# Attention and GEGLU in one kernel: padding fills and normalisation tails moved to GpSimd, three reorderings in the first block, and another form of the closing test

## The chip, the cores and the metric

The kernel runs on one core of a Trainium2 chip. The metric is the device time of one execution in microseconds (us). The engines are called as the profile has them: PE is TensorE, DVE VectorE, ACT ScalarE, POOL GpSimd, SP SyncE, whose queue issues nearly all DMAs.

## The reference

The input x has 2048 rows of 448, all in bf16. It is normalised row by row and goes through two branches whose results are added to it.

```python
xn = layernorm(x)
# A: 16 heads of 28, causal sliding window of 256 keys
q, k, v = split(xn @ wqkv)
p = softmax(where(0 <= i - j < 256, q @ k.T * 28 ** -0.5, -1e9))
# B: F = 1792
h = gelu(xn @ w_gate) * (xn @ w_up)
return x + (p @ v) @ wo + h @ w_down
```

## The kernel before

The rows are worked on in four query blocks (qb 0 to 3) of 512 rows, that is four tiles of 128 rows each. A block goes through attention, then through the gate and up projections (`gated`), and its down projections, to which the attention's output projection is added in the same PSUM tile, run inside the next block's attention. The order of all instructions is written out by hand: the program emits them one after another, and each engine takes its own in that order. While PE works on a block's attention, generators (`Feed`, `share`) put the projections of the next block and other matmuls in between, by a cost in ns that each yields.

Block 0 is special, since nothing is there yet when it begins. Its attention has twelve steps, three for each of the four head groups g. A step computes scores on PE, takes their Exp on ACT (`p_sb`), and zeroes the parts outside the window with selects on POOL (`masked`). A group's PV product (`pv(g)`) comes ahead of the scores of steps 4, 7 and 10, and after the last step for the fourth group; it needs the masked `p_sb` of that group's three steps. The score tile is single-buffered here (`score_pool(1)`), so a step's scores wait until the Exp before them has read it.

Between block 0's steps stand the q and k projections of groups 1 to 3 (`gen_qk`), the last two v tiles of the block, early up projections, and block 1's projections. A list `aux` has one entry for each step: normalisation of tiles 4 to 7 and their DMA transposes (`ahead`, `ahead2`, `ahead3`), then `fill_pads`, then statistics of tiles 8 to 11. `stat` computes mean and variance on DVE, `rstd` the reciprocal root on ACT as Exp(-0.5 Ln), `norm` scales a tile in two pieces, 448 columns and a copy of the last 64 (the tail).

The contraction of 448 is three chunks of 128 and a half chunk of 64. The half chunks of two products use both halves of PE's rows and run side by side: q with k (`qk_halves`, weights `w3p`), and v of two tiles (`v_half`).

Heads have 28 columns in places of 32. In the free four columns of the padded weights `wqp`, `wkp` and `w3p` the later blocks compute the keys of head group 3; `fill_pads` writes the weights for that, by twelve copies of 16 or 48 elements a partition and a memset.

The PV product also gives the row sums of the softmax. `sums` transposes them into rows, copies them into `l_all` and takes their reciprocal; `inverse` transposes that back, and `scale_o` multiplies on POOL. At the end the program tests that all sums lay within 1e-18 and 1e18, adds the 128 partitions' answers up in a matmul (`nok`), and reads the count as a register of every engine; a second, general path would run if it were not 128. That matmul, the copy of its result and the register load stand among the last block's down projections.

Of the kernel before, what the change touches and what calls it, by code (L numbers as in the profile page):

```python
# [9 lines left out]
ALU = mybir.AluOpType  # L10
AX = mybir.AxisListType
bf16 = mybir.dt.bfloat16
f32 = mybir.dt.float32
i32 = mybir.dt.int32

S, D, H, Dh, F = 2048, 448, 16, 28, 1792
P = 128
NT = S // P
NF = F // P
QB, NB = 512, 4  # L20
SCALE = float(Dh) ** -0.5
L_LO, L_HI = 1e-18, 1e18


HOLD = True
# [29 lines left out]
def share(feeds, first, second):  # L55

    want = [first, second]
    while True:
        can = [i for i, f in enumerate(feeds) if f.gens and want[i] > 190 and not f.held]
        if not can:  # L60
            return
        i = max(can, key=lambda i: (not feeds[i].closed, want[i]))
        for f in feeds:
            if f is not feeds[i]:
                f.closed = False
        want[i] -= feeds[i].run()


def drain(feeds):

    while any(f.gens for f in feeds):
        min((f for f in feeds if f.gens), key=lambda f: (f.held, f.closed)).run()
# [3 lines left out]
def kernel(  # L76
# [11 lines left out]
    nc = tc.nc  # L88
    const = ctx.enter_context(tc.tile_pool(name="const", bufs=1))
# [3 lines left out]
    work = fast.enter_context(tc.tile_pool(name="work", bufs=3))  # L93
# [3 lines left out]
    phase = [None]  # L97
# [84 lines left out]
    kT = const.tile([P, 4, S], bf16, name="kT")  # L182
    mv_all = const.tile([P, NT, 2], f32, name="mv_all")
    rstd_all = const.tile([P, NT], f32, name="rstd_all")
    l_all = const.tile([P, NB * 4, 16], f32, name="l_all")

    def warmup(n):
        wps = phase[0].pool.tile([P, 2, QB], f32, name="wps", tag="s")
# [9 lines left out]
    def rstd(t, n):  # L198
        lnv = work.tile([P, 4], f32, name="lnv")
        nc.scalar.activation(out=lnv[:, 0:n], in_=mv_all[:, t:t + n, 1], func=ACT.Ln, bias=eps_t[:, 0:1], scale=1.0)  # L200
        nc.scalar.activation(out=rstd_all[:, t:t + n], in_=lnv[:, 0:n], func=ACT.Exp, scale=-0.5)
# [3 lines left out]
    def norm(t):  # L205
        xn = work.tile([P, 4, P], bf16, name="xn", bufs=4)
        xf = xn[:, :, :].rearrange("p a b -> p (a b)")
        for eng, lo, n, src in ((nc.vector, 0, D, 0), (nc.gpsimd if t in (1, 2) else nc.vector, D, 64, 384)):
            eng.tensor_scalar(out=xf[:, lo:lo + n], in0=x_sb[:, t, src:src + n], scalar1=mv_all[:, t, 0:1],
                              scalar2=rstd_all[:, t:t + 1], op0=ALU.subtract, op1=ALU.mult)  # L210
        xns[t] = xn
# [38 lines left out]
    def v_half(t, pv):  # L250
        mm_half(pv, xnT[:, 3, t * P:(t + 1) * P], wv[:, 3, :], t % 2, False, True)
# [22 lines left out]
    def qk_halves(qb, g, pq, pk):  # L274
        w3 = w3p[:, 4 * g:4 * g + 4, :].rearrange("p h d -> p (h d)")
        for hi, ps in enumerate((pq, pk)):
            mm_half(ps, w3, xnT[:, 3, qb * QB:(qb + 1) * QB], hi, False, True)
# [7 lines left out]
    def gen_qk(qb, gs, others=()):  # L285

        for g in gs:
            pq = bank("pq")[:, :]
            proj(pq, wqp, qb, g)
            if qb and g == 3:  # L290
                yield 650
                ts = slice(qb * QB, (qb + 1) * QB)
                nc.tensor.matmul(pq, lhsT=w3p[:, 12:16, :].rearrange("p h d -> p (h d)"), rhs=xnT[:, 3, ts], start=False, stop=True,
                                 skip_group_check=True)
                nc.scalar.copy(out=qT[:, 3, ts], in_=pq)
                done.add((qb, 3))
                yield -220
                return
            yield 650
            pk = bank("pk")[:, :]  # L300
            proj(pk, wkp, qb, g)
            yield 650, HOLD
            qk_halves(qb, g, pq, pk)
            for t, pv in others:
                v_half(t, pv)
            if others:
                v_copy(*others[1], nc.vector.tensor_copy)
            qk_copies(qb, g, pq, pk)
            others = ()
            yield -360  # L310

    def fill_pads(last):


        def put(dst, src, n, lo):

            src = src.rearrange("p (j d) -> p j d", d=Dh)[:, :, lo:]
            if n == 4:
                nc.vector.tensor_copy(out=dst[:, 12:16, Dh:32], in_=src[:, :, 24:28])
            src = src[:, :, 0:24].rearrange("p j (g i) -> p g j i", i=8)[:, :, :, 0:4]  # L320
            nc.vector.tensor_copy(out=dst[:, 0:12, Dh:32].rearrange("p (g j) i -> p g j i", j=4), in_=src)

        if not last:
            for c in range(3):
                k = wraw[:, c, D + 12 * Dh:2 * D]
                put(wqp[:, c, :, :], k, 4, 0)
                put(wkp[:, c, :, :], k, 3, 4)
            return
        put(w3p[0:64, :, :], w3k[0:64, :], 4, 0)
        put(w3p[64:128, :, :], w3k[64:128, :], 3, 4)  # L330
        nc.vector.memset(w3p[64:128, 12:16, :], 0.0)

    k3 = dram.tile([4, 7, 4, QB], bf16, name="k3")

# [17 lines left out]
    DOWN = 4 * 3400  # L352
# [178 lines left out]
    def attention(qb, feeds, aux, plan):  # L531
# [7 lines left out]
        def sums():  # L539

            g, oc = copied.pop(0)
            l1 = work.tile([P, 16, 32], f32, name="l1", tag="wc", bufs=1)
            ls = l_all[:, 4 * qb + g, :]
            nc.vector.transpose(out=l1[:, :, :].rearrange("p a b -> p (a b)"), in_=oc[:, :])  # L544
            nc.vector.tensor_copy(out=ls, in_=l1[:, :, Dh])
            ri = work.tile([P, 16], f32, name="ri")
            nc.vector.reciprocal(out=ri[:, :], in_=ls)
            inverses.append((g, oc, ri, l1))

        def inverse():  # L550

            g, oc, ri, l1 = inverses.pop(0)
            rb = l1 if qb else work.tile([P, 16, 32], f32, name="rb", tag="wb", bufs=1)
            nc.vector.transpose(out=rb[:, :, :], in_=ri[:, :].unsqueeze(2).to_broadcast([P, 16, 32]))  # L554
            later.append((g, oc, rb[:, :, :].rearrange("p a b -> p (a b)")))

        def add_halves(oc, ov):
# [33 lines left out]
        for i, (scores, ncol, edges) in enumerate(steps):  # L591
# [18 lines left out]
            for g, half, kt, q0, nq, col in scores:  # L610
                k0, nk = (64 * half, 64) if half is not None else (0, P)
                for j in range(4):
                    r = slice(32 * j, 32 * j + Dh)
                    nc.tensor.matmul(ss[k0:k0 + nk, j, col:col + nq], lhsT=kT[r, g, kt * P + k0:kt * P + k0 + nk],  # L614
                                     rhs=qT[r, g, qb * QB + q0:qb * QB + q0 + nq], start=True, stop=True,
                                     tile_position=(32 * j, k0), skip_group_check=True)
                parts.setdefault(g, []).append((half, kt, q0, nq, col, p_sb))
            nc.scalar.activation(out=p_sb[:, :, 0:ncol], in_=ss[:, :, 0:ncol], func=ACT.Exp, scale=SCALE)  # L618
            flush()
            if qb:  # L620
# [106 lines left out]
    def ahead2():  # L727
        stat(6)
        stat(7)
        rstd(6, 2)  # L730
        norm(5)
        dma_transp(5)

# [74 lines left out]

    g1 = work.tile([P, 512], f32, name="g1", tag="wc", bufs=1)
    g2 = work.tile([P, 512], f32, name="g2", tag="wb", bufs=1)  # L810
    okc = const.tile([P, 1], f32, name="okc")
    okb = const.tile([P, 1], bf16, name="okb")
    one = const.tile([P, 1], bf16, name="one")
    lf = l_all[:, :, :].rearrange("p a b -> p (a b)")
    nc.vector.memset(one[:, :], 1.0)
    nc.vector.tensor_scalar(out=g1[:, 0:256], in0=lf, scalar1=L_LO, scalar2=None, op0=ALU.is_ge)
    nc.vector.scalar_tensor_tensor(out=g2[:, 0:256], in0=lf, scalar=L_HI, in1=g1[:, 0:256], op0=ALU.is_le, op1=ALU.mult)
    nc.vector.tensor_reduce(out=okc[:, :], in_=g2[:, 0:256], axis=AX.X, op=ALU.min)
    nc.vector.tensor_copy(out=okb[:, :], in_=okc[:, :])
    feed = Feed((gen_down(NB - 1, "dmomd" if last_tag[0] == "o" else "omdmo"), DOWN))  # L820
    share([feed], DOWN / 3, 0)
    nok = phase[0].pool.tile([P, 2 * QB], f32, name="nok", tag="s")
    nc.tensor.matmul(nok[0:1, 0:1], lhsT=okb[:, :], rhs=one[:, :], start=True, stop=True)
    flag = const.tile([1, 1], i32, name="flag")
    nc.vector.tensor_copy(out=flag[:, :], in_=nok[0:1, 0:1])
    share([feed], DOWN / 3, 0)
    n_ok = nc.values_load(flag[0:1, 0:1], min_val=0, max_val=P)
    drain([feed])
    phase[0].close()
    fast.close()  # L830


    with tc.If(n_ok < P, preferred_fallthrough_block=True, label="general"):
        general_path(tc, locals_=dict(x_sb=x_sb, xnT=xnT, qT=qT, kT=kT, v_sb=v_sb, wg=wg, wu=wu, wgu3=wgu3, wd=wd, wo=wo,
                                      ident=ident, outv=outv))

# [108 lines left out]
```

## Time and profile before

| | us |
|---|---|
| median of 3 runs | 222.42 |
| lowest and highest | 222.25, 222.54 |
| the profiled execution | 222.38 |
| its span | 220.7 |
| PE busy | 210.7 (95%) |
| DVE busy | 156.2 (71%) |
| ACT busy | 133.3 (60%) |
| POOL busy | 44.7 (20%) |

The span goes from the first instruction to the last; what lies around it belongs to the time. Busy shares are means over the span. The program is one long pipeline with a start of some 12 us, in which the first tiles come in and are normalised.

### The profile page before, as it was taken

The numbers are of one execution on the slowest core, as the hardware profiler recorded it, in microseconds if no ns is written. First come the engines' busy times: TensorE is split into PE (matmuls) and PEld (weight loads), VectorE is DVE, ScalarE is ACT, GpSimd is POOL, SyncE is SP. The second block draws the span as 40 slices with busy tenths as digits, with TensorE's granted clock in tenths as the row PEclk, the third lists the DMA queues.
The fourth block names the chain that finished last, engine by engine and source line by source line (L and its number), as shares of the span: only waits on it lengthen the run. The fifth ranks groups of instructions, "written<-read, shape, count | busy, mean of one in ns | idle before, by whom it ended". The sixth has DMA issues, their size and how long they took to land.

```text
span 220.7 us, 5415 instructions
## 1 busy us (share of the span) xinstructions
PE 210.7 (95%) x2257; PEld 95.2 (43%) x2282; DVE 156.2 (71%) x370; ACT 133.3 (60%) x131; POOL 44.7 (20%) x65
## 2 busy tenths in 40 slices
PE   6899999999999999999999999999999999999992
PEld 1333333443444454434444445443344445444472
DVE  5989996799666993679565796396345899579320
ACT  3587788662878875432878887233576777564000
POOL 5763687320000120022000022022000022022000
PEclk9999999999999999999999999999999999999999
DMA  6999799203200001102300000200000000000010
GB/s 190 283 296 98 142 344 301 66 1 73 46 0 24 24 24 27 20 0 47 72 1 24 23 0 24 50 16 0 0 4 21 24 3 24 24 1 0 22 46 25
DMA packets 18045, 13.30 MB, mean 60 GB/s; under 512 B 8704, under 2 KB 16992, under 8 KB 18016
## 3 DMA queue, kind: packets, MB, share of 16 engines
q1 hardware_dynamic: 17072, 12.62, 22.7%
q8 instruction: 19, 0.31, 0.6%
q10 hardware_dynamic: 944, 0.29, 0.5%
q14 instruction: 10, 0.08, 0.2%
HBM read 9.15 MB, written 2.18 MB: 51 GB/s over the span
## 4 chain that ended last, share of the span: by engine, by line
PE 91%; DVE 4%; DMA 1%; issue 1%; ACT 0%
PE po L376 20%; PE gt L228 15%; PE u L228 12%; PE sc L614 6%; PE po L371 6%; PE gt L234 5%; PE ue L228 5%; PE ov L574 5%; PE pq L228 4%; PE pv L228 4%; PE pk L228 3%; PE pq L234 2%; DVE st L195 2%; PE g L228 1%; DMA x_sb<-in_A_x_dram 1%
## 5 line engine op out<-in xcount | busy, mean ns | idle before, releaser
L618 ACT ACTIVATE p_sb<-sc 128x2048 bf16<-128x2048 f32 (+2 forms) x42 | 73.8, 1758 | 12.6 <-PE sc L614 7.2
L376 PE MATMUL po<-wd,hT 128*128 128x448 bf16 (+1 forms) x238 | 50.0, 342 | 0.0
L459 ACT ACTIVATE ge<-gt 128x1024 bf16<-128x1024 f32 x26 | 26.6, 1024 | 34.9 <-PE u L234 20.1
L537 POOL TENSOR_TENSOR oN<-oc,l 128x512 bf16<-128x512 f32 x12 | 16.0, 1332 | 137.5 <-DVE l L554 87.2
L228 PE MATMUL gt<-xnT,wg 128*128 128x512 bf16 x149 | 36.1, 379 | 1.0 <-issue 1.0
L466 DVE TENSOR_TENSOR hT<-ge,u 128x512 bf16<-128x512 bf16 x40 | 25.7, 682 | 11.9 <-ACT ge L459 11.8
L376 PEld LDWEIGHTS <-hT 128*128 128x128 bf16 x238 | 21.4, 98 | 18.6 <-issue 2.6
L228 PE MATMUL u<-xnT,wu 128*128 128x512 bf16 x116 | 29.0, 379 | 0.2
L518 DVE TENSOR_TENSOR p_sb<-p_sb,masks 128x256 bf16<-128x256 bf16 (+1 forms) x90 | 27.3, 357 | 0.4 <-ACT p_sb L618 0.4
L228 PEld LDWEIGHTS <-wg 128*128 128x128 bf16 x168 | 15.3, 98 | 21.3 <-issue 4.5
L228 PEld LDWEIGHTS <-wu 128*128 128x128 bf16 x168 | 16.0, 98 | 19.2 <-issue 1.0
L559 DVE TENSOR_TENSOR oc<-oc,ov 128x512 f32<-128x512 f32 x12 | 8.2, 687 | 15.2 <-ACT oc L558 15.2
L614 PE MATMUL sc<-qT,kT 28*64 28x320 bf16 (+7 forms) x640 | 16.9, 263 | 0.1
L381 DVE TENSOR_TENSOR res<-po,x_sb 128x448 bf16<-128x448 f32 (+1 forms) x17 | 10.0, 586 | 8.8 <-PE po L376 8.7
L371 PE MATMUL po<-wo,oN 128*128 128x448 bf16 (+1 forms) x68 | 15.9, 342 | 0.0
L528 POOL TENSOR_SCALAR_AFFINE_SELECT p_sb<-p_sb 128x512 bf16<-128x512 bf16 (+1 forms) x20 | 14.2, 731 | 8.3 <-ACT p_sb L618 8.1
L410 DVE CAST hT<-ue 128x512 bf16<-128x512 f32 x16 | 10.2, 680 | 6.3 <-PE ue L234 6.2
L234 PE MATMUL gt<-xnT,wgu 64*128 64x512 bf16 (+1 forms) x67 | 12.7, 380 | 0.0
L228 PE MATMUL pq<-xnT,wqp 128*128 128x512 bf16 x36 | 11.7, 380 | 0.7 <-DVE v_sb L254 0.3
L558 ACT COPY oc<-ov 128x512 f32<-128x512 f32 x12 | 7.0, 584 | 8.8 <-PE ov L574 8.8
L544 DVE STREAM_TRANSPOSE l<-oc 128x512 f32<-128x512 f32 x16 | 11.3, 705 | 1.4 <-POOL oN L537 1.2
L228 PE MATMUL ue<-xnT,wu 128*128 128x512 bf16 x43 | 11.6, 380 | 0.4 <-issue 0.2
(91 smaller groups left out, 242.5 us busy)
## 6 DMA issues: line engine op xcount, KB each, us to landing
out_dram<-res SPq DMA_DIRECT2D x15, 112.0 KB
x_sb<-in_A_x_dram SPq DMA_DIRECT2D x3, 448.0 KB
wu<-in_B_w_up_dram SPq DMA_DIRECT2D x1, 1344.0 KB
wg<-in_B_w_gate_dram SPq DMA_DIRECT2D x1, 1344.0 KB
wd<-in_B_w_down_dram SPq DMA_DIRECT2D x3, 448.0 KB
wraw<-in_A_wqkv_dram SPq DMA_DIRECT2D x2, 252.0 KB
wo<-in_A_wo_dram SPq DMA_DIRECT2D x4, 98.0 KB
wv<-in_A_wqkv_dram SPq DMA_DIRECT2D x1, 336.0 KB
```

Of the source, the lines that this page charges most:

```text
L228: nc.tensor.matmul(ps, lhsT=lhs(c), rhs=rhs(c), start=start and c == 0, stop=stop and c == 2, skip_group_check=True)
L234: nc.tensor.matmul(ps[c:c + m], lhsT=lhs[p0:p0 + 64, c:c + m], rhs=rhs[p0:p0 + 64], start=start, stop=stop, tile_position=(p0, c), skip_gr ...
L371: nc.tensor.matmul(po[:, 0:w], lhsT=oN[:, g, cs], rhs=wo[:, g, lo:up], start=(g == 0), stop=False, skip_group_check=True)
L376: nc.tensor.matmul(po[:, 0:w], lhsT=hT[:, f, cs], rhs=wd[:, f, lo:up], start=False, stop=(f == NF - 1), skip_group_check=True)
L459: nc.scalar.activation(out=ge[:, :, :], in_=pr["gt"][:, :, :], func=ACT.Gelu_apprx_tanh)
L466: nc.vector.tensor_tensor(out=hT[:, f + i, :], in0=ge[:, i, :], in1=u, op=ALU.mult)
L518: nc.vector.tensor_tensor(out=reg, in0=reg, in1=m, op=ALU.mult)
L528: nc.gpsimd.affine_select(out=reg, in_=reg, pattern=mid + [[1 if diag else -1, min(w, P)]], compare_op=ALU.is_ge, fill=0.0, base=0 if diag ...
L537: nc.gpsimd.tensor_tensor(out=oN[:, g, :], in0=oc[:, :], in1=inv, op=ALU.mult)
L544: nc.vector.transpose(out=l1[:, :, :].rearrange("p a b -> p (a b)"), in_=oc[:, :])
L614: nc.tensor.matmul(ss[k0:k0 + nk, j, col:col + nq], lhsT=kT[r, g, kt * P + k0:kt * P + k0 + nk], rhs=qT[r, g, qb * QB + q0:qb * QB + q0 + ...
L618: nc.scalar.activation(out=p_sb[:, :, 0:ncol], in_=ss[:, :, 0:ncol], func=ACT.Exp, scale=SCALE)
```

## The change

- `norm`: the 64-column tails of tiles 5, 6 and 7 go from DVE to POOL, as those of tiles 1 and 2 are already.
- `gen_qk`: the two v halves stand ahead of the q/k halves.
- `fill_pads`: all twelve copies and the memset go from DVE to POOL. In POOL's order nine copies come between the masks of steps 3 and 4, three copies and the memset between those of steps 4 and 5.
- `rstd(6, 2)` moves from the `aux` entry after step 1 to just before the Exp of step 2; in ACT's order the copy of q of group 2 now stands ahead of it.
- `sums`: the reciprocal reads the transposed sums directly and is kept (`inv_all`, in place of `l_all`); the copy goes. The test at the end is made on the reciprocals, with the same bounds.
- The end: the minimum over the partitions is taken on DVE (a transpose, two reductions, four copies of one element, one reduction, a cast) in place of the matmul, all ahead of the last block's down projections. The scratch tiles are zeroed after them.

```diff
-        for eng, lo, n, src in ((nc.vector, 0, D, 0), (nc.gpsimd if t in (1, 2) else nc.vector, D, 64, 384)):
+        for eng, lo, n, src in ((nc.vector, 0, D, 0), (nc.gpsimd if t in (1, 2, 5, 6, 7) else nc.vector, D, 64, 384)):
...
-            qk_halves(qb, g, pq, pk)
             for t, pv in others:
                 v_half(t, pv)
+            qk_halves(qb, g, pq, pk)
             if others:
                 v_copy(*others[1], nc.vector.tensor_copy)
             qk_copies(qb, g, pq, pk)
...
             if n == 4:
-                nc.vector.tensor_copy(out=dst[:, 12:16, Dh:32], in_=src[:, :, 24:28])
+                nc.gpsimd.tensor_copy(out=dst[:, 12:16, Dh:32], in_=src[:, :, 24:28])
             src = src[:, :, 0:24].rearrange("p j (g i) -> p g j i", i=8)[:, :, :, 0:4]
-            nc.vector.tensor_copy(out=dst[:, 0:12, Dh:32].rearrange("p (g j) i -> p g j i", j=4), in_=src)
+            nc.gpsimd.tensor_copy(out=dst[:, 0:12, Dh:32].rearrange("p (g j) i -> p g j i", j=4), in_=src)
...
-        nc.vector.memset(w3p[64:128, 12:16, :], 0.0)
+        nc.gpsimd.memset(w3p[64:128, 12:16, :], 0.0)
...
-            ls = l_all[:, 4 * qb + g, :]
             nc.vector.transpose(out=l1[:, :, :].rearrange("p a b -> p (a b)"), in_=oc[:, :])
-            nc.vector.tensor_copy(out=ls, in_=l1[:, :, Dh])
-            ri = work.tile([P, 16], f32, name="ri")
-            nc.vector.reciprocal(out=ri[:, :], in_=ls)
-            inverses.append((g, oc, ri, l1))
+            nc.vector.reciprocal(out=inv_all[:, 4 * qb + g, :], in_=l1[:, :, Dh])
+            inverses.append((g, oc, l1))
...
+            if not qb and i == 2:
+                rstd(6, 2)
             nc.scalar.activation(out=p_sb[:, :, 0:ncol], in_=ss[:, :, 0:ncol], func=ACT.Exp, scale=SCALE)
...
     def ahead2():
         stat(6)
         stat(7)
-        rstd(6, 2)
         norm(5)
         dma_transp(5)
...
-    nc.vector.tensor_copy(out=okb[:, :], in_=okc[:, :])
+    nc.vector.transpose(out=okt, in_=okc)
+    nc.vector.tensor_reduce(out=okm, in_=okt, axis=AX.X, op=ALU.min)
+    for i in range(4):
+        nc.vector.tensor_copy(out=okr[0:1, i:i + 1], in_=okm[32 * i:32 * i + 1, :])
+    nc.vector.tensor_reduce(out=ok1, in_=okr, axis=AX.X, op=ALU.min)
+    nc.vector.tensor_copy(out=flag[:, :], in_=ok1)
     feed = Feed((gen_down(NB - 1, "dmomd" if last_tag[0] == "o" else "omdmo"), DOWN))
-    share([feed], DOWN / 3, 0)
-    nok = phase[0].pool.tile([P, 2 * QB], f32, name="nok", tag="s")
-    nc.tensor.matmul(nok[0:1, 0:1], lhsT=okb[:, :], rhs=one[:, :], start=True, stop=True)
-    flag = const.tile([1, 1], i32, name="flag")
-    nc.vector.tensor_copy(out=flag[:, :], in_=nok[0:1, 0:1])
-    share([feed], DOWN / 3, 0)
-    n_ok = nc.values_load(flag[0:1, 0:1], min_val=0, max_val=P)
+    share([feed], DOWN * 2 / 3, 0)
+    n_ok = nc.values_load(flag[0:1, 0:1], min_val=0, max_val=1)
     drain([feed])
+    for g in (g1, g2):
+        nc.vector.memset(g[:, :], 0.0)
```

More of the change, by code (lines that the diff above doesn't have):

```diff
@@ L21 @@
 SCALE = float(Dh) ** -0.5
-L_LO, L_HI = 1e-18, 1e18
+INV_LO, INV_HI = 1e-18, 1e18
 HOLD = True
@@ L184 @@
     rstd_all = const.tile([P, NT], f32, name="rstd_all")
-    l_all = const.tile([P, NB * 4, 16], f32, name="l_all")
+    inv_all = const.tile([P, NB * 4, 16], f32, name="inv_all")
     def warmup(n):
@@ L542, in sums @@
             l1 = work.tile([P, 16, 32], f32, name="l1", tag="wc", bufs=1)
-            ls = l_all[:, 4 * qb + g, :]
             nc.vector.transpose(out=l1[:, :, :].rearrange("p a b -> p (a b)"), in_=oc[:, :])
-            nc.vector.tensor_copy(out=ls, in_=l1[:, :, Dh])
-            ri = work.tile([P, 16], f32, name="ri")
-            nc.vector.reciprocal(out=ri[:, :], in_=ls)
-            inverses.append((g, oc, ri, l1))
+            nc.vector.reciprocal(out=inv_all[:, 4 * qb + g, :], in_=l1[:, :, Dh])
+            inverses.append((g, oc, l1))
         def inverse():
-            g, oc, ri, l1 = inverses.pop(0)
+            g, oc, l1 = inverses.pop(0)
             rb = l1 if qb else work.tile([P, 16, 32], f32, name="rb", tag="wb", bufs=1)
-            nc.vector.transpose(out=rb[:, :, :], in_=ri[:, :].unsqueeze(2).to_broadcast([P, 16, 32]))
+            nc.vector.transpose(out=rb[:, :, :], in_=inv_all[:, 4 * qb + g, :].unsqueeze(2).to_broadcast([P, 16, 32]))
             later.append((g, oc, rb[:, :, :].rearrange("p a b -> p (a b)")))
@@ L810 @@
     g2 = work.tile([P, 512], f32, name="g2", tag="wb", bufs=1)
[L811 to L817, printed above, removed]
@@ L818 @@
-    nc.vector.tensor_reduce(out=okc[:, :], in_=g2[:, 0:256], axis=AX.X, op=ALU.min)
-    nc.vector.tensor_copy(out=okb[:, :], in_=okc[:, :])
-    feed = Feed((gen_down(NB - 1, "dmomd" if last_tag[0] == "o" else "omdmo"), DOWN))
-    share([feed], DOWN / 3, 0)
-    nok = phase[0].pool.tile([P, 2 * QB], f32, name="nok", tag="s")
-    nc.tensor.matmul(nok[0:1, 0:1], lhsT=okb[:, :], rhs=one[:, :], start=True, stop=True)
-    flag = const.tile([1, 1], i32, name="flag")
-    nc.vector.tensor_copy(out=flag[:, :], in_=nok[0:1, 0:1])
@@ L826 @@
-    share([feed], DOWN / 3, 0)
-    n_ok = nc.values_load(flag[0:1, 0:1], min_val=0, max_val=P)
+    okc, okt, okm, okr, ok1 = g1[:, 256:288], g1[:, 288:320], g1[:, 320:321], g1[0:1, 324:328], g1[0:1, 328:329]
+    flag = const.tile([1, 1], i32, name="flag")
+    lf = inv_all[:, :, :].rearrange("p a b -> p (a b)")
+    nc.vector.memset(okc, 1.0)
+    nc.vector.tensor_scalar(out=g1[:, 0:256], in0=lf, scalar1=INV_LO, scalar2=None, op0=ALU.is_ge)
+    nc.vector.scalar_tensor_tensor(out=g2[:, 0:256], in0=lf, scalar=INV_HI, in1=g1[:, 0:256], op0=ALU.is_le, op1=ALU.mult)
@@ new lines @@
+    nc.vector.tensor_reduce(out=okc[:, 0:1], in_=g2[:, 0:256], axis=AX.X, op=ALU.min)
+    nc.vector.transpose(out=okt, in_=okc)
[4 more added lines that the diff above has]
+    nc.vector.tensor_copy(out=flag[:, :], in_=ok1)
+    feed = Feed((gen_down(NB - 1, "dmomd" if last_tag[0] == "o" else "omdmo"), DOWN))
@@ L828 @@
+    share([feed], DOWN * 2 / 3, 0)
+    n_ok = nc.values_load(flag[0:1, 0:1], min_val=0, max_val=1)
     drain([feed])
+    for g in (g1, g2):
+        nc.vector.memset(g[:, :], 0.0)
     phase[0].close()
     fast.close()
-    with tc.If(n_ok < P, preferred_fallthrough_block=True, label="general"):
+    with tc.If(n_ok < 1, preferred_fallthrough_block=True, label="general"):
         general_path(tc, locals_=dict(x_sb=x_sb, xnT=xnT, qT=qT, kT=kT, v_sb=v_sb, wg=wg, wu=wu, wgu3=wgu3, wd=wd, wo=wo,
```

## The prediction

> **What bounds the kernel now.** I read the profile's page first: span, busy shares, and the chain of work that ended last.
>
> ```profile
> span 220.7 us, 5415 instructions
> PE 210.7 (95%) x2257; PEld 95.2 (43%) x2282; DVE 156.2 (71%) x370; ACT 133.3 (60%) x131; POOL 44.7 (20%) x65
> PE 91%; DVE 4%; DMA 1%; issue 1%; ACT 0%
> ```
>
> TensorE (PE) is busy 95% of the span and is 91% of the chain. So an edit on another engine is worth something only where PE waits for that engine, or begins to. The busy time in windows says where PE has any idle time left.
>
> ```profile
> 0.00:20.00 20.00, 16.18 (x96) 5.96 (x97) 16.14 (x47) 12.31 (x25) 12.42 (x34) 1.00 0.91 235
> 20.00:30.00 10.00, 9.89 (x91) 3.89 (x90) 9.75 (x30) 8.30 (x8) 6.03 (x8) 1.00 0.85 154
> ```
>
> The columns after the window and its length are PE, PEld, DVE, ACT, POOL (busy us and instructions), granted clock, DMA share, GB/s. From 20 us on PE is busy 99% of the time, at the full clock. The first 20 us hold 3.8 us of PE idle time; the change touches nothing of it before the first steps of block 0's attention, so I look there. The timeline of PE, ACT and DVE there, put in order of time (columns: start, duration, engine, line, operation; in brackets the idle time and who ended it):
>
> ```profile
> 14.27 0.39 PE L234 MATMUL pq<-xnT,w3p 64*128 64x512 bf16 x1
> 14.50 0.35 PE L234 MATMUL pv<-wv,xnT 64*128 64x448 bf16 x2
> 14.89 0.62 DVE L254 CAST v_sb<-pv 128x448 bf16<-128x448 f32 x1 [0.39 <-PE pv L234]
> 15.57 0.81 PE L228 MATMUL pq<-xnT,wqp 128*128 128x512 bf16 x3 [0.26 <-DVE v_sb L254]
> 16.22 0.81 PE L228 MATMUL pk<-xnT,wkp 128*128 128x512 bf16 x3
> 15.35 1.45 ACT L618 ACTIVATE p_sb<-sc 128x1536 bf16<-128x1536 f32 x1
> 16.96 0.39 PE L234 MATMUL pq<-xnT,w3p 64*128 64x512 bf16 x1
> 17.50 0.82 PE L228 MATMUL pq<-xnT,wqp 128*128 128x512 bf16 x3
> 17.63 0.29 ACT L200 ACTIVATE lnv<-mv_all,eps_t 128x2 f32<-128x2 f32 x1 [0.82 <-DVE mv_all L196]
> 17.96 0.20 ACT L201 ACTIVATE rstd_all<-lnv 128x2 f32<-128x2 f32 x1
> 18.07 0.57 ACT L281 CAST qT<-pq 128x512 bf16<-128x512 f32 x1
> 18.53 1.03 ACT L618 ACTIVATE p_sb<-sc 128x1024 bf16<-128x1024 f32 x1
> 18.68 0.81 PE L228 MATMUL pk<-xnT,wkp 128*128 128x512 bf16 x3 [0.36 <-ACT qT L281]
> 19.75 0.40 PE L614 MATMUL sc<-qT,kT 28*128 28x128 bf16 x8
> ```
>
> Two waits are seen. The projection at 15.57 waits for VectorE's copy of v out of its PSUM bank. The one at 18.68 waits for ACT's copy of q, which was free to start when its sums were complete (16.96 + 0.39 = 17.35) but stood in ACT's queue behind the logarithm and exponential, which in turn waited for VectorE's statistics until 17.63.
>
> **The change part by part.** *v halves first.* Today the q/k halves go at 14.27 and the v halves at 14.50, so v comes out 0.23 us sooner when the pairs are exchanged. VectorE is idle then (0.39 in the bracket), so its copy starts at 14.66 and the projection goes 0.23 us sooner, at 15.34. The k copy comes behind the v copy anyway and gains as much. No queue of another engine is passed.
>
> *q copy ahead of Ln/Exp.* In the new order the q copy starts when its halves end, at 17.35 - 0.23 = 17.12, and ends at 17.70. The projection it releases would, without a wait, follow its predecessor after three matmuls, 0.65 (15.57 to 16.22). So it can start at 17.50 - 0.23 + 0.65 = 17.92 in place of 18.68: 0.76 sooner, 0.53 of it from this edit. But then scores of step 3, at 19.75, meet the next limit: they need the single score buffer, which step 2's Exp must have read. Queued behind the q copy are now Ln, Exp and then step 2's Exp. Ln starts when the q copy lets go (17.12 + 0.46, the spacing from 18.07 to 18.53) or soon after the statistics are in, about 17.6, as now; step 2's Exp starts 0.11 behind the second small one, at 18.1, and ends at 19.1. Step 3's scores start at 19.15: of the 0.76, 0.16 goes into this wait and **0.60** stays. Tiles 6 and 7 get their scale at the same time as now.
>
> *Tail.* The old check ends in a small matmul in the midst of the last down projections.
>
> ```profile
> 202.53 0.92 PE L371 MATMUL po<-wo,oN 128*128 128x448 bf16 x4
> 205.93 0.92 PE L371 MATMUL po<-wo,oN 128*128 128x448 bf16 x4
> 207.16 0.16 PE L823 MATMUL nok<-one,okb 128*1 128x1 bf16 x1
> 209.54 0.92 PE L371 MATMUL po<-wo,oN 128*128 128x448 bf16 x4
> 205.06 0.16 DVE L819 CAST okb<-okc 128x1 bf16<-128x1 f32 x1
> 216.59 0.39 DVE L381 TENSOR_TENSOR res<-po,x_sb 128x224 bf16<-128x224 f32 x1 [1.33 <-PE po L376]
> 1.18 0.81 DVE L167 MEMSET wo<- 128x896 uint32 x1 [0.16 <-issue]
> ```
>
> A tile of four plus fourteen matmuls takes 205.93 - 202.53 = 3.40; the one with the small matmul inside takes 209.54 - 205.93 = 3.61. Its removal gives **0.21**. The nine small VectorE steps that stand in place of that cast and of the copy of the flag cost below 3 us together if each takes up to twice the cast's 0.16; they begin at 205.06 and delay at most the first result, whose bank PE wants again only for the last half tile, over 4 us later. The two scratch memsets come behind the last result (216.59 + 0.39). At 0.81 for 896 words a 512-word one is 0.46, so VectorE is done at 217.9, while the last output is on its way and the span ends at 220.7: nothing, by the cover of that transfer. Were that cover not there, 0.9.
>
> *No copy of the sums.* Sixteen VectorE copies go, in places where PE waits for nobody: nothing.
>
> *Padding fills and tails on POOL.* VectorE loses work that PE never waits for: no gain. POOL's queue, though, is in order, and the masks that PE needs are in it. Fill and masks, with the matmul that waits for them last:
>
> ```profile
> 22.28 1.69 POOL L528 TENSOR_SCALAR_AFFINE_SELECT p_sb<-p_sb 128x1024 bf16<-128x1024 bf16 x2 [1.94 <-ACT p_sb L618]
> 24.31 1.23 POOL L528 TENSOR_SCALAR_AFFINE_SELECT p_sb<-p_sb 128x512 bf16<-128x512 bf16 x2 [0.35 <-ACT p_sb L618]
> 25.89 0.63 POOL L528 TENSOR_SCALAR_AFFINE_SELECT p_sb<-p_sb 128x512 bf16<-128x512 bf16 x1 [0.35 <-ACT p_sb L618]
> 28.07 0.67 PE L574 MATMUL ov<-p_sb,v_sb 128*32 128x128 bf16 x16
> ```
>
> These are the masks of steps 3, 4 and 5 (head group 1), and the PV product of that group. Nine fill copies now stand between the first two rows, three copies and a memset between the second and third. POOL would be through at 23.97 + 1.23 + 0.63 = 25.83 plus the fills; PE wants it at 28.07: room 2.24. Since step 3's Exp comes 0.7 sooner (its q copy no longer waits) and PE 0.6, the room is about 2.34. What the fills take beyond it, PE stands still, and nothing later gives it back, as PE has no idle time there.
>
> No copy runs on POOL in this trace. The nearest rows:
>
> ```profile
> L161 POOL TENSOR_SCALAR_AFFINE_SELECT masks<-masks 64x64 bf16<-64x64 bf16 x18 | 4.2, 238 | 0.8
> 8.79 0.52 POOL L161 TENSOR_SCALAR_AFFINE_SELECT masks<-masks 64x64 bf16<-64x64 bf16 x2
> 9.36 0.44 POOL L161 TENSOR_SCALAR_AFFINE_SELECT masks<-masks 64x64 bf16<-64x64 bf16 x2
> L209 POOL TENSOR_SCALAR xn<-x_sb,mv_all,rstd_all 128x64 bf16<-128x64 bf16 x2 | 1.3, 649 | 2.9 <-ACT rstd_all L201 2.9
> masks.py:197 POOL MEMSET ident<- 128x128 bf16 x1 | 0.2, 204 | 0.3 <-POOLq L929 0.3
> L929 POOL MEMSET const-float32-0.0<- 128x1 f32 x1 | 0.1, 98 | 0.3 <-issue 0.3
> L321 DVE COPY wqp<-wraw 128x48 bf16<-128x48 bf16 x3 | 0.5, 166 | 0.0
> ```
>
> The copies have 48 or 16 elements a partition. A 64-element select takes 0.24, and a pair on the same 64 partitions takes 0.44, so they start 0.20 apart; a pair that changes the partitions takes 0.52, 0.28 apart. The lower end is a one-element memset, 0.10; the upper end the two-scalar operation of line 209, 0.65. I take 0.20: the select also reads one operand and writes it, and the scalars of line 209 are what a copy does not have. Twelve copies and a memset of 0.20 make 2.6; **the stall is 2.6 - 2.34 = 0.26**. At the lower end the sum is 1.4 and there is none; at the upper end 8.0, a stall of 5.7.
>
> [...]
>
> The tails of tiles 5 to 7 delay DMA transposes in SP's queue, and behind those the weight loads.
>
> ```profile
> 18.46 4.30 SPq L215 DMA_TRANSPOSE xnT<-xn  x2
> 19.75 3.02 SPq L215 DMA_TRANSPOSE xnT<-xn  x1
> 26.53 1.31 PE L228 MATMUL pv<-wv,xnT 128*128 128x448 bf16 x6
> ```
>
> The tail of tile 5 comes behind the masks of step 1 and costs up to 0.65, so the transpose goes some 0.3 late. The third transpose holds SP for 3.02 us, until 22.77, though its input is long there; the tails of 6 and 7 (1.3 together, behind step 2's mask) are done by 21.7, so the fourth still goes at 22.8. PE reads those tiles from 26.53 on. Nothing; if that hold is not there to hide it, up to 1 us of lateness against over 2 us of room.
>
> **The sum.** 0.60 + 0.21 - 0.26 = 0.55 off. The profiled execution took 222.38 (span 220.7 and 1.68 around it); 222.38 - 0.55 = 221.83. The median of the runs, 222.42, is 0.04 above it: **221.9 us**.
>
> **The rivals.** The result hangs on one price, that of a POOL copy. Below 0.21 each the stall is under 0.37 and the kernel gains over 0.44 us, 0.2%, about the least that a measurement of this kernel can tell. From 0.21 to 0.28 it is within that. Above 0.28 it is slower.
>
> *POOL becomes the bound (slower).* [...] Against: the selects. It decides from 0.28 on. Chance 0.25.
>
> *The gains cancel (no change).* Copies at 0.21 to 0.28, up to the pace of the selects that change partitions, give a stall of 0.4 to 1.2: 222.0 to 222.8. So does a q copy whose gain turns wholly into the wait for the score buffer. Chance 0.28.
>
> *No stall at all.* Copies under 0.18 leave 222.42 - 0.81 = 221.6; this lies in the forecast's own case, faster, whose chance is 0.47.
>
> **The numbers.** The likeliest case gives 221.9, itself 221.6 to 222.0. The range goes from 221.4 (the first wait vanishes wholly, 0.1 more, and small VectorE gains) to 223.2, a copy just under twice VectorE's price; beyond lie 0.15. Faster 0.47, same 0.28, slower 0.25.
>
> **What would show it.** Right: no bracket at the projections that now stand at 15.57 and 18.68, a small new one before step 3's scores, ended by ACT; fill copies near 0.20; PE waiting 0.1 to 0.4 before the PV product near 27.5, ended by POOL; equal 3.40 us tiles at the end; the last 4 us unchanged. Wrong: fill copies of 0.3 or more with a PE wait of over 1 us there; a PE wait for a transpose near 26; or an end that waits for VectorE's memsets.

## The result, and the profile after

Median of six runs each, taken together: 222.48 us before (222.25 to 222.72), 221.67 us changed (221.25 to 221.75). The ratio is 0.9964, interval 0.9953 to 0.9974: the kernel is 0.81 us faster. Run once more beside other experiments it was 221.51 against 222.51, ratio 0.9955 (0.9937 to 0.9973). The profiled execution of the changed kernel took 221.75.

The page first: span, busy shares, the chain.

```profile
span 220.0 us, 5437 instructions
PE 213.2 (97%) x2281; PEld 95.8 (44%) x2281; DVE 153.1 (70%) x346; ACT 133.3 (61%) x131; POOL 48.0 (22%) x81
PE 93%; DVE 3%; DMA 1%; ACT 1%; issue 0%; DVEq 0%
```

PE is still the chain. Its busy time is not to be compared with that of before: before lists 2257 matmuls beside 2282 weight loads, so some 25 matmul records are missing there. What can be compared is where single instructions stand. The timeline of PE, DVE and ACT at the start of block 0, put in order of time:

```profile
14.34 0.36 PE L234 MATMUL pv<-wv,xnT 64*128 64x448 bf16 x2
14.75 0.62 DVE L254 CAST v_sb<-pv 128x448 bf16<-128x448 f32 x1
15.43 0.81 PE L228 MATMUL pq<-xnT,wqp 128*128 128x512 bf16 x3
17.23 0.59 ACT L281 CAST qT<-pq 128x512 bf16<-128x512 f32 x1 [0.34 <-PE pk L234]
17.72 0.30 ACT L200 ACTIVATE lnv<-mv_all,eps_t 128x2 f32<-128x2 f32 x1
18.01 0.81 PE L228 MATMUL pk<-xnT,wkp 128*128 128x512 bf16 x3
18.16 1.00 ACT L617 ACTIVATE p_sb<-sc 128x1024 bf16<-128x1024 f32 x1
18.76 0.39 PE L234 MATMUL pq<-xnT,w3p 64*128 64x512 bf16 x1
19.21 0.40 PE L611 MATMUL sc<-qT,kT 28*128 28x128 bf16 x8
```

Both brackets at the projections are gone (15.43 and 18.01). ACT copies q first, then come Ln and the Exp of step 2. Next, the timeline of POOL where the fills now stand, with the two PE rows that follow:

```profile
21.62 1.69 POOL L528 TENSOR_SCALAR_AFFINE_SELECT p_sb<-p_sb 128x1024 bf16<-128x1024 bf16 x2 [0.62 <-ACT p_sb L617]
23.25 0.20 POOL L319 COPY wqp<-wraw 128x16 bf16<-128x16 bf16 x1
24.47 0.22 POOL L321 COPY wkp<-wraw 128x48 bf16<-128x48 bf16 x1
24.64 1.22 POOL L528 TENSOR_SCALAR_AFFINE_SELECT p_sb<-p_sb 128x512 bf16<-128x512 bf16 x2
25.82 0.19 POOL L319 COPY w3p<-w3k 64x16 bf16<-64x16 bf16 x1
26.66 0.63 POOL L528 TENSOR_SCALAR_AFFINE_SELECT p_sb<-p_sb 128x512 bf16<-128x512 bf16 x1
27.53 0.67 PE L571 MATMUL ov<-p_sb,v_sb 128*32 128x128 bf16 x16
28.14 0.34 PE L611 MATMUL sc<-qT,kT 28*128 28x384 bf16 x4
```

A copy takes 0.19 to 0.22, but the next starts before it has ended: the nine copies between the first two masks hold POOL for 24.64 - 23.25 = 1.39, that is about 0.155 each. The three copies and the memset take 26.66 - 25.82 = 0.84. The last mask ends at 27.29, the PV product starts at 27.53 and has no bracket: no stall.

The end, from PE's and DVE's timelines:

```profile
205.32 0.92 PE L371 MATMUL po<-wo,oN 128*128 128x448 bf16 x4
208.73 0.92 PE L371 MATMUL po<-wo,oN 128*128 128x448 bf16 x4
205.61 0.14 DVE L821 CAST flag<-g 1x1 int32<-1x1 f32 x1
216.23 1.03 DVE L827 MEMSET g<- 128x512 f32 x2
```

The tile that held the small matmul takes 3.41 in place of 3.61. The flag is ready at 205.75; the kernel reads it only behind two thirds of these down projections. The memsets end at 217.26, 2.7 before the span does: hidden.

**Two marks.** The single parts are worth 0.2 to 0.4 us each. That is about as much as two profiled executions of the changed kernel differ in: the first scores start at 12.60 in one and at 12.38 in the other, and behind block 0's fourth PV product another 0.3 lies between them. So beside the times (medians; a ratio is worked out from all runs, not from the two medians) I use a mark that leaves both out: from the first score matmul to the start of block 0's fourth PV product. Its two rows in the kernel before, then in the changed one:

```profile
12.53 0.40 PE L614 MATMUL sc<-qT,kT 28*128 28x128 bf16 x8
41.80 0.67 PE L574 MATMUL ov<-p_sb,v_sb 128*32 128x128 bf16 x16
```

```profile
12.60 0.40 PE L611 MATMUL sc<-qT,kT 28*128 28x128 bf16 x8
41.27 0.68 PE L571 MATMUL ov<-p_sb,v_sb 128*32 128x128 bf16 x16
```

| kernel | mark (us) | PE waits between 14 and 30 us | median less that of before (us) |
|---|---|---|---|
| before | 29.27 | 0.26 and 0.36 | 0 |
| changed; again | 28.67; 28.67 | none | -0.81; -1.00 |
| e1 fills on DVE | 28.67 | none | -0.64 |
| e2 q/k halves first | 28.89 | 0.27 | -0.61 |
| e3 Ln/Exp ahead of the q copy | 29.05 | 0.36 | -0.44 |
| e4 old closing test | 28.66 | none | -0.76 |
| e5 first fills twice | 29.51 | 0.65 | -0.05 |
| e6 reorderings without the moves to POOL | 30.09 | 0.58 and 0.58 | +0.37 |
| e7 Ln/Exp behind step 2's Exp | 28.53 | none | -1.00 |
| e8 moves to POOL alone | 29.27 | 0.27 and 0.36 | -0.19 |
| e9 closing test with four matmuls | 28.82 | 0.20 | -0.29 |
| e10 e6 with Ln/Exp behind step 2's Exp | 30.44 | 1.33 and 0.31 | +0.86 |
| e11 e6 with the fills ahead of the mask | 29.00 | 0.21 | -0.38 |

The mark fell by 0.60 and the last tile by 0.20: 0.80 of the 0.81. The mark is not wholly free of scatter either: e9's edit lies at the other end of the program, and its mark is 0.15 longer than the changed kernel's, by a wait of 0.20 for a v copy. A difference of 0.15 between two marks needs its own row as evidence.

### The profile page after: what moved, and what is told of

Same layout as the page of the kernel before. It is cut to its first block, busy times and chain, and to the rows that moved or that the text cites. A ratio compares the mean times of both kernels' runs of the same rounds, so it can differ in the third digit from the quotient of the medians.

```text
span 220.0 us, 5437 instructions
## 1 busy us (share of the span) xinstructions
PE 213.2 (97%) x2281; PEld 95.8 (44%) x2281; DVE 153.1 (70%) x346; ACT 133.3 (61%) x131; POOL 48.0 (22%) x81
## 4 chain that ended last, share of the span: by engine, by line
PE 93%; DVE 3%; DMA 1%; ACT 1%; issue 0%; DVEq 0%
PE po L376 20%; PE gt L228 16%; PE u L228 12%; PE sc L611 6%; PE po L371 6%; PE gt L234 5%; PE ue L228 5%; PE ov L571 5%; PE pq L228 4%; PE pv L228 4%; PE pk L228 3%; PE pq L234 1%; PE g L228 1%; DMA x_sb<-in_A_x_dram 1%; PE ue L234 1%; PE pv L234 1%
## 5 line engine op out<-in xcount | busy, mean ns | idle before, releaser
L228 PE MATMUL gt<-xnT,wg 128*128 128x512 bf16 x156 | 37.5, 380 | 0.0
L518 DVE TENSOR_TENSOR p_sb<-p_sb,masks 128x256 bf16<-128x256 bf16 (+1 forms) x90 | 26.8, 352 | 0.4 <-ACT p_sb L617 0.4
L228 PE MATMUL pq<-xnT,wqp 128*128 128x512 bf16 x45 | 12.2, 380 | 0.1
```

Of the source, the lines that this page charges most:

```text
L228: nc.tensor.matmul(ps, lhsT=lhs(c), rhs=rhs(c), start=start and c == 0, stop=stop and c == 2, skip_group_check=True)
L518: nc.vector.tensor_tensor(out=reg, in0=reg, in1=m, op=ALU.mult)
```

## The experiments

### The three gains, each undone alone

Experiment e2 puts the q/k halves back ahead of the v halves:

```diff
+            qk_halves(qb, g, pq, pk)
             for t, pv in others:
                 v_half(t, pv)
-            qk_halves(qb, g, pq, pk)
```

> The changed kernel with the q/k halves ahead of the v halves again. Theory A: the PE wait for VectorE's v copy comes back, 0.2 us in the projection that follows, and the time is 0.6 us under the kernel before. Theory B: the wait is hidden behind step 3's wait for the score buffer, and the time stays 0.8 under it.

Measured: 221.82 us, ratio 0.9969 (0.9957 to 0.9981). Experiment e3 puts the Ln/Exp of tiles 6 and 7 back ahead of the q copy:

```diff
     def ahead2():
         stat(6)
         stat(7)
+        rstd(6, 2)
...
-            if not qb and i == 2:
-                rstd(6, 2)
             nc.scalar.activation(out=p_sb[:, :, 0:ncol], in_=ss[:, :, 0:ncol], func=ACT.Exp, scale=SCALE)
```

> The changed kernel with Ln and Exp of tiles 6 and 7 back in their old place ahead of the q copy. Theory A: the projection of k waits for ACT's q copy again, step 3's scores go 0.4 us later, and the time is 0.4 us under the kernel before. Theory B: with VectorE relieved its statistics are in earlier, so Ln and Exp are done before the q copy is due and at most 0.1 is lost.

Measured: 221.99 us, ratio 0.9975 (0.9963 to 0.9988). From PE's timelines, the first row from e2, the second from e3:

```profile
15.64 0.81 PE L228 MATMUL pq<-xnT,wqp 128*128 128x512 bf16 x3 [0.27 <-DVE v_sb L254]
18.58 0.81 PE L228 MATMUL pk<-xnT,wkp 128*128 128x512 bf16 x3 [0.36 <-ACT qT L281]
```

Each undoing brings back its own wait and no other, and the mark grows by 0.22 and by 0.38, together 0.60. The times point the same way, but their intervals hold more than one reading; the waits and the marks decide.

Experiment e4 takes back the old closing test, with its matmul, and leaves the memsets out:

```diff
-    nc.vector.transpose(out=okt, in_=okc)
...
+    nc.tensor.matmul(nok[0:1, 0:1], lhsT=okb[:, :], rhs=one[:, :], start=True, stop=True)
...
-    for g in (g1, g2):
-        nc.vector.memset(g[:, :], 0.0)
```

> The changed kernel with the closing test's sum over the partitions in a matmul again and no scratch memsets. Theory A: the tile of down projections with that matmul takes 3.61 us in place of 3.40, and the time is 0.6 us under the kernel before. Theory B: the memsets or the longer VectorE chain had cost something at the end, so that 0.1 or less is lost.

Measured: 221.67 us against 222.43, ratio 0.9956 (0.994 to 0.9972). By its time alone the matmul costs nothing, but in that profile the first scores came 0.21 earlier than in the changed kernel's. So e9, otherwise as e4, makes the same matmul four times over, two down-projection matmuls after each:

```diff
+    for _ in range(4):
+        nc.tensor.matmul(nok[0:1, 0:1], lhsT=okb[:, :], rhs=one[:, :], start=True, stop=True)
+        share([feed], 400, 0)
```

> The changed kernel with the matmul test, its one-column matmul made four times, each with two down projection matmuls behind it. Theory A (each such matmul costs PE 0.2 us): the tile with them takes 4.2 us in place of 3.40, and the time is 0.0 to 0.1 us over the kernel before. Theory B (the gap is a wait for the bank or the operand of the first one): the tile takes 3.6 to 3.7 us, and the time is 0.6 us under the kernel before.

Measured: 222.15 us against 222.44, ratio 0.9991 (0.9982 to 1.0). PE's timeline of e9, the beginnings of the tile with the four matmuls and of the next:

```profile
205.25 0.92 PE L371 MATMUL po<-wo,oN 128*128 128x448 bf16 x4
209.46 0.92 PE L371 MATMUL po<-wo,oN 128*128 128x448 bf16 x4
```

4.21 in place of 3.41 is 0.20 for each matmul; e4's one made its tile 3.60. So the cost of 0.2 each is shown in the traces. The whole time came lower than I had expected, 0.29 under the kernel before where I had put it 0.0 to 0.1 over. The profiled execution took 222.38, as that of before; why the median lies lower is not shown. The times of e4 and e9 by themselves do not show the price of one matmul.

### How much room POOL has

Experiment e5 writes the first nine fills twice:

```diff
-            for c in range(3):
+            for c in (0, 1, 2) * 2:
```

> The changed kernel with the nine first fill copies on POOL made twice. Theory A (the fills are hidden only up to a room of about 0.24 us that is left before the second PV product): nine more copies at 0.16 take 1.4 us, PE waits 1.2 us for POOL's mask there, and the time is 0.4 us over the kernel before. Theory B (PE does not wait for this queue): no wait, and 0.8 us under the kernel before.

Measured: 222.39 us against 222.44, ratio 0.9998 (0.9989 to 1.0007). POOL's and PE's timelines of e5:

```profile
23.06 0.20 POOL L319 COPY wqp<-wraw 128x16 bf16<-128x16 bf16 x1
25.85 1.23 POOL L528 TENSOR_SCALAR_AFFINE_SELECT p_sb<-p_sb 128x512 bf16<-128x512 bf16 x2
27.87 0.64 POOL L528 TENSOR_SCALAR_AFFINE_SELECT p_sb<-p_sb 128x512 bf16<-128x512 bf16 x1
27.34 0.56 PE L571 MATMUL ov<-p_sb,v_sb 128*32 128x128 bf16 x12
28.56 0.29 PE L571 MATMUL ov<-p_sb,v_sb 128*32 128x256 bf16 x4 [0.65 <-POOL p_sb L528]
28.79 0.34 PE L611 MATMUL sc<-qT,kT 28*128 28x384 bf16 x4
```

Eighteen copies take 25.85 - 23.06 = 2.79, so nine more cost 1.40, at the same 0.155 each. The PV product starts on time at 27.34 and runs twelve of its sixteen matmuls; only the last four wait, for the mask of step 5 (27.87 + 0.64). From the start of the PV product to the next scores it is 1.45 in place of 0.61: PE is 0.84 later. So 1.40 - 0.84 = 0.56 was still free in the changed kernel. I had expected a longer wait: my room ended where the PV product starts, but the last mask is wanted only by its last quarter. The other term is confirmed: added time on POOL beyond the room does become PE time.

### Are the moves to POOL worth anything?

Experiment e8 keeps the moves to POOL and the missing copy of the sums, and takes back both reorderings (the diff has two in the first block, where the title counts three) and the closing test, that is the edits of e2, e3 and e4 together:

> The kernel before with the moves to POOL and without the copy of the sums, but with the old order of v halves and of Ln and Exp and the old matmul test. Theory A: no gain, as PE's waits for the v copy and the q copy are all there; the fills end just in time for the second PV product, so the time is that of the kernel before, within 0.15 us. Theory B (relief of VectorE is worth something by itself): 0.2 to 0.4 us under it.

Measured: 222.25 us against 222.44, ratio 0.9987 (0.9978 to 0.9996). The mark is 29.27, as before, and both old waits (0.27, 0.36) are there. The time is 0.19 under the kernel before, a little more than the 0.15 that I had allowed. The profiled execution took 222.53, more than that of before, so the trace does not show where the 0.19 comes from: it stays open. The moves alone bring nothing that the mark shows.

Experiment e1 puts only the fills back on DVE:

```diff
-                nc.gpsimd.tensor_copy(out=dst[:, 12:16, Dh:32], in_=src[:, :, 24:28])
+                nc.vector.tensor_copy(out=dst[:, 12:16, Dh:32], in_=src[:, :, 24:28])
...
-            nc.gpsimd.tensor_copy(out=dst[:, 0:12, Dh:32].rearrange("p (g j) i -> p g j i", j=4), in_=src)
+            nc.vector.tensor_copy(out=dst[:, 0:12, Dh:32].rearrange("p (g j) i -> p g j i", j=4), in_=src)
...
-        nc.gpsimd.memset(w3p[64:128, 12:16, :], 0.0)
+        nc.vector.memset(w3p[64:128, 12:16, :], 0.0)
```

> The changed kernel with the padding fills back on VectorE. Theory A (the gain is three PE waits removed; the fills cost nothing on either engine): as the changed kernel, 0.8 us under the kernel before, within 0.15; no new PE wait. Theory B (the relief of VectorE carries part of the gain): the fills delay VectorE's casts out of PSUM, PE waits for a bank between 21 and 24 us, and 0.3 to 0.7 us of the gain are lost.

Measured: 221.79 us against 222.43, ratio 0.9962 (0.995 to 0.9975); mark 28.67, no wait. Up to here the moves looked superfluous. Experiment e6 puts the fills and the tails of tiles 5 to 7 back on DVE: e1's edit and

```diff
-        for eng, lo, n, src in ((nc.vector, 0, D, 0), (nc.gpsimd if t in (1, 2, 5, 6, 7) else nc.vector, D, 64, 384)):
+        for eng, lo, n, src in ((nc.vector, 0, D, 0), (nc.gpsimd if t in (1, 2) else nc.vector, D, 64, 384)):
```

> The changed kernel with both the padding fills and the tails of tiles 5 to 7 back on VectorE: v halves, Ln/Exp order, sums and closing test stay changed. Theory A (the moves to POOL are worth nothing by themselves): PE goes from block 0's first scores to its fourth PV product in the changed kernel's time, and the whole is 0.8 us under the kernel before. Theory B (VectorE's relief is needed for the reorderings to pay): VectorE's statistics or casts are late, PE waits 0.2 us or more in the first block, and 0.2 to 0.5 us of the gain are lost.

Measured: 222.88 us against 222.51, ratio 1.0015 (1.0006 to 1.0025): slower than the kernel before, though both reorderings and the new closing test are in. First two of the nine fills in the kernel before, the seventh and the last, then DVE's, POOL's and PE's timelines of e6:

```profile
21.91 0.16 DVE L319 COPY wqp<-wraw 128x16 bf16<-128x16 bf16 x1
22.07 0.16 DVE L321 COPY wkp<-wraw 128x48 bf16<-128x48 bf16 x1
```

```profile
21.44 0.16 DVE L321 COPY wkp<-wraw 128x48 bf16<-128x48 bf16 x1
21.52 1.00 DVE L319 COPY wqp<-wraw 128x16 bf16<-128x16 bf16 x1
22.43 0.17 DVE L321 COPY wqp<-wraw 128x48 bf16<-128x48 bf16 x1
22.60 1.27 DVE L410 CAST hT<-ue 128x512 bf16<-128x512 f32 x2
24.40 0.42 DVE L319 COPY w3p<-w3k 64x16 bf16<-64x16 bf16 x1
21.40 1.10 POOL L528 TENSOR_SCALAR_AFFINE_SELECT p_sb<-p_sb 128x1024 bf16<-128x1024 bf16 x1 [1.75 <-ACT p_sb L617]
23.57 1.23 POOL L528 TENSOR_SCALAR_AFFINE_SELECT p_sb<-p_sb 128x512 bf16<-128x512 bf16 x2 [0.49 <-ACT p_sb L617]
23.33 0.81 PE L228 MATMUL ue<-xnT,wu 128*128 128x512 bf16 x3 [0.58 <-DVE hT L410]
25.93 0.73 PE L228 MATMUL pv<-wv,xnT 128*128 128x448 bf16 x3 [0.58 <-DVE hT L410]
```

In the kernel before, the nine fills were over at 22.23, and the mask of step 3 began on POOL at 22.28 (a row that the prediction shows): they missed each other by 0.05. The reorderings bring the Exp of step 3, and with it that mask, 0.88 sooner, to 21.40, but the fills only by 0.39 (the seventh, at 21.91 there, begins at 21.52 here); 0.14 of both is the earlier start of that execution. Now this copy of 16 elements that begins at 21.52 takes 1.00 in place of 0.16: it ends at 22.52, with the first select (21.40 + 1.10 = 22.50). DVE's casts of `ue` stand behind it, PE wants their bank and waits 0.58. At 24.40 another fill takes 0.42 in place of 0.15 and ends at 24.82, with the second select of its pair (23.57 + 1.23 = 24.80). PE waits 0.58 once more, and these 0.27 are only part of it: DVE's queue is late there anyway, and e10, whose fill at this place takes 0.15, still waits 0.31. It is 1.16 in all, and the mark is 1.42 longer than the changed kernel's.

The copies of line 319, four rows of four elements on both sides, are held by the selects (1.00 at 21.52, 0.42 at 24.40), while one of line 321, twelve rows of four, takes 0.17 at 22.43, beside the second select of the pair. No run here shows what makes the difference. Nor does every POOL instruction hold the copies of line 319: in e1, those that ran beside POOL's line 209 (its row is shown further down) took 0.15 to 0.23.

Two rivals were open: the hold (a DVE copy stands still until POOL's select ends), or simply too much work on DVE. Experiment e11 keeps all work of e6 on DVE and moves only the first nine fills ahead of step 3's k copy, so that they end before the mask begins:

```diff
         v_copy(2, pvs[2], nc.vector.tensor_copy)
+        fill_pads(False)
         loads()
...
-                aux = [ahead, ahead2, ahead3, lambda: fill_pads(False), lambda: fill_pads(True), lambda: None,
+                aux = [ahead, ahead2, ahead3, lambda: None, lambda: fill_pads(True), lambda: None,
```

> As the run with the reorderings only (fills and tails on VectorE), with the nine first fill copies ahead of VectorE's copy of k of group 3 in place of behind it. In that run one of these copies of 16 elements took 1.00 us where the others took 0.16; it stood beside POOL's select of step 3, which began at 21.40, and PE then waited twice 0.58 us for VectorE's casts. Theory A (the copy is held while POOL's select runs): here the nine are done by 21.2, ahead of that select, all take 0.15 to 0.23, PE waits 0.0 to 0.2 us in sum, and the time is 0.6 to 0.8 us under the kernel before. Theory B (VectorE simply has too much work there): the work is the same, so PE waits about 1 us as before, and the time is 0.2 to 0.5 us over the kernel before.

Measured: 221.91 us against 222.29, ratio 0.998 (0.9964 to 0.9996). DVE's, POOL's and PE's timelines of e11:

```profile
21.09 0.16 DVE L321 COPY wkp<-wraw 128x48 bf16<-128x48 bf16 x1
21.40 1.69 POOL L528 TENSOR_SCALAR_AFFINE_SELECT p_sb<-p_sb 128x1024 bf16<-128x1024 bf16 x2 [1.74 <-ACT p_sb L617]
24.84 0.73 PE L228 MATMUL pv<-wv,xnT 128*128 128x448 bf16 x3 [0.21 <-DVE hT L410]
```

With the same work on the same engine, PE's waits fall from 1.16 to 0.21 and the mark from 30.09 to 29.00. So 1.09 of the 1.42 goes with the hold. The other 0.33 is left with the same work on DVE: the k copy stands behind the fills, the casts of `ue` come later, and one wait of 0.21 remains; that part is the load. The time gained 0.38 where I had expected 0.6 to 0.8; the interval, 0.1 to 0.8, holds both. In e1 the hold is absent for the same reason: without the tails of tiles 5 to 7, DVE comes to the fills sooner. Its first and last, before POOL's mask at 21.61, and POOL's tails beside them:

```profile
20.11 0.17 DVE L319 COPY wqp<-wraw 128x16 bf16<-128x16 bf16 x1
20.83 0.16 DVE L321 COPY wkp<-wraw 128x48 bf16<-128x48 bf16 x1
19.86 1.13 POOL L209 TENSOR_SCALAR xn<-x_sb,mv_all,rstd_all 128x64 bf16<-128x64 bf16 x2
```

### The wait for the score buffer

Experiment e7 puts the Ln/Exp of tiles 6 and 7 behind step 2's Exp:

```diff
+            nc.scalar.activation(out=p_sb[:, :, 0:ncol], in_=ss[:, :, 0:ncol], func=ACT.Exp, scale=SCALE)
             if not qb and i == 2:
                 rstd(6, 2)
-            nc.scalar.activation(out=p_sb[:, :, 0:ncol], in_=ss[:, :, 0:ncol], func=ACT.Exp, scale=SCALE)
```

> The changed kernel with Ln and Exp of tiles 6 and 7 moved once more, behind step 2's Exp. Theory A (step 3's scores wait for step 2's Exp, which stands behind these two): step 3's scores go 0.13 us sooner still, the transposes of tiles 6 and 7 follow 1 us later without PE noticing, and the time is 0.9 to 1.0 us under the kernel before. Theory B: the step behind is bound by the q copy or the DMA transposes, and the time is as the changed kernel's or up to 0.5 us longer.

Measured: 221.44 us against 222.44, ratio 0.9954 (0.9941 to 0.9968). PE's timeline of e7, the half chunks and step 3's scores:

```profile
18.54 0.39 PE L234 MATMUL pq<-xnT,w3p 64*128 64x512 bf16 x1
18.86 0.40 PE L611 MATMUL sc<-qT,kT 28*128 28x128 bf16 x8
```

The scores follow the halves after 0.32; in the changed kernel it is 19.21 - 18.76 = 0.45. So PE did lose 0.13 there to the single score buffer, in a wait too short for a bracket, and the mark of e7 is 0.14 shorter. Its time is the lowest of all, but no interval here tells it from the changed kernel's.

Experiment e10 does the same to e6 (the edits of e6 and e7 together):

> As the run with the reorderings only, with Ln and Exp of tiles 6 and 7 behind step 2's Exp. Theory A: the 0.15 us of the earlier run with that order are had without POOL's help too, 0.9 to 1.0 us under the kernel before. Theory B: with the tails on VectorE behind the late Ln and Exp, VectorE's copies of v and k of that place are late, PE waits for a bank, and the time is the changed kernel's or longer.

Measured: 223.37 us against 222.51, ratio 1.0038 (1.0026 to 1.0051). DVE's and PE's timelines:

```profile
21.46 1.08 DVE L319 COPY wqp<-wraw 128x16 bf16<-128x16 bf16 x1
22.63 0.51 DVE L319 COPY wqp<-wraw 128x16 bf16<-128x16 bf16 x1
23.95 0.81 PE L228 MATMUL ue<-xnT,wu 128*128 128x512 bf16 x3 [1.33 <-DVE hT L410]
```

With the scale of tiles 6 and 7 later, their normalisation and the fills behind it are later too, and two fills of the nine are held in place of one. They end at 22.54 and 23.14; POOL's two selects beside them end at 22.52 and 23.11. An edit that takes 0.14 off the mark with the moves adds 0.35 to it without them, and 0.5 to the time.

The changed kernel was run again beside these:

> The changed kernel once more, beside the next two on the same chip. Profiled executions so far reach the first scores of block 0 between 12.38 and 12.64 us, which is as much as single parts of the change are worth. If that scatter belongs to the execution and not to the kernel, this one is again 0.8 us under the kernel before, within 0.2 us, and may reach the first scores at another time than 12.59.

Its result stands at the top; its mark is the same to the hundredth.

## Why the prediction was right, and where it was not

- **v halves first** (0.23): right. The wait is gone, and e2 brings back 0.27 of wait and 0.22 of mark.
- **q copy ahead of Ln/Exp** (0.53, of which 0.16 goes to the score buffer): right, 0.38 by e3, and 0.13 to the score buffer by e7. The sum of both, forecast as 0.60, measures 0.60 by the mark.
- **Tail** (0.21): right, 0.20 by the tiles and by e9. The memsets are hidden, as said; together they take 1.03.
- **Copy of the sums, tails to POOL** (nothing): nothing is seen of them when no reordering is made (e8); no run takes away the copy of the sums alone. PE waits for no transpose: from 12 us on the changed kernel's trace lists no wait of PE.
- **Stall by the fills** (0.26): wrong, there is none, and this is the 0.2 by which the time came under the forecast. Two terms were mis-sized. The thirteen small steps cost POOL 1.39 + 0.84 = 2.23, not 2.6, as a copy follows the one before it after 0.155. And the room ended at the wrong place: the last mask is wanted by the last quarter of the PV product, and e5 shows 0.56 left. The first alone was enough: the last mask ended 0.24 before the product began.
- **POOL becomes the bound**: not borne out. The upper end of the range, 223.2, stood for a copy of just under twice VectorE's price; no run shows such a copy. On POOL a copy took 0.19 to 0.23 (changed kernel, e5); one of 48 elements took 0.22 there and 0.16 on DVE, a ratio of 1.4. The pace, 0.155 against about 0.08 (DVE's copies at 21.44 and 21.52 in e6), stands near two, but 0.155 is under the 0.20 that the forecast took.
- **"VectorE loses work that PE never waits for: no gain."** Wrong as a step, though the sum did not show it. It was read from the trace of before, where the fills ended 0.05 ahead of the mask. The reorderings move the mask onto them. With neither move to POOL the change comes out 0.37 over before (e6) in place of 0.81 under it: the cover that they give is worth 1.2 us. That the sum came out all the same is luck on this point: the moves that it set at nothing were made together with the reorderings that need them. The move of the tails is enough for it (e1); whether that of the fills alone would be was not run.

## What to carry to other kernels

When an edit lets one engine go sooner, look what it then runs beside on the other engines: a gap of 0.05 us in the old trace is no cover. Undo the parts of a change in combinations, not only one at a time: here the moves to POOL brought nothing that the mark shows when made alone (e8), that of the fills cost nothing to undo (e1), and with neither of them the whole gain was lost (e6). And when room in a queue is reckoned, follow the consumer to the very instruction that needs the last piece, and take the pace at which small steps follow each other, not the time that one takes.

## What the runs showed of the hardware

- Four copies of 16 elements a partition on DVE that began with 0.40 us or more of a select on POOL still to run took 1.00, 1.08, 0.51 and 0.42 us (e6, e10), and each ended 0.02 to 0.03 after that select. One that began 0.01 ahead of a select took 0.15 beside it (e11). Where no POOL instruction ran such a copy took 0.15 to 0.16, beside POOL's line 209 0.15 to 0.23 (e1). Copies of 48 elements in another pattern took 0.16 to 0.17 beside the same selects (e6, e10).
- Copies of 16 and 48 elements on POOL took 0.19 and 0.22 in the mean and started 0.155 apart in the mean (changed kernel, e5).
- A matmul of one column between matmuls of 448 cost PE 0.19 in e4 and 0.20 in e9; its own row in e4 has 0.16.
- The same program's first scores came at 12.60 in one execution and at 12.38 in another. A part worth 0.2 us is better judged by a mark inside the trace, and by the row of its own wait, than by the time.
